# A two-layer expert stage with its first layer turned round: tokens on partitions, 512 weight columns as the moving operand, rows transposed by DMA

## The chip, the cores and the metric

The kernel runs on one core of a Trainium2 chip. Its engines are TensorE (PE: matmuls, with PEld for the weight loads), VectorE (DVE), ScalarE (ACT), GpSimd (POOL) and SyncE (SP). Each works through its own instructions in order and waits on semaphores that other engines or DMAs raise. DMAs are issued from the queues of SP, ACT and POOL; a DMA transpose is issued from SP here. A matmul multiplies a stationary operand (at most 128 x 128, the "weights" of the instruction, lhsT) with a moving operand of up to 512 columns (rhs), and adds into a PSUM bank of 512 fp32 columns. The metric is the device time of one execution in microseconds.

## What is computed

Attention over 4 batches, 8 heads, 768 positions and 64 dimensions per head is followed by a mixture of 4 experts. Three heads attend to all earlier positions, five to 4 sink positions and a window of 64. The 3072 x 512 result, one row per token, goes through every expert:

```python
p = domain_probs / (domain_probs.sum(-1, keepdims=True) + 1e-09)
out = np.zeros((N, D), dtype=np.float32)          # N = 3072 tokens, D = 512
for e in range(E):                                # E = 4 experts, F = 1024
    h = np.maximum(x @ w1[e], 0.0)                # layer 1: 512 -> 1024
    out += p[:, e:e + 1] * (h @ w2[e])            # layer 2: 1024 -> 512
```

Since a probability is positive, p * max(h, 0) = max(p * h, 0): the probability may be applied before the second layer. Both kernels do that in the stage that the change touches.

## The kernel before

Tokens are handled in 24 tiles of 128. Attention works in 8 groups of three tiles (half a batch each, `attention(b, c)`) and leaves its result transposed, in `xT[g]`: model dimension on partitions (4 chunks of 128), tokens on the free axis. Attention of the first group runs alone. Then `moe_steps` is a generator of expert work, and a loop at the end of the kernel weaves steps of the remaining attention between its steps by a plan of spent time. All engines' orders are as the program emits them; nothing is reordered by a scheduler.

Tiles 0 to 3 go through the experts in a plain way. The other 20 tiles go in ten *pairs* (`pair_steps`), and these pairs are the subject here. A pair has 256 tokens.

*Layer 1 before.* The hidden units are put on partitions: the stationary operand is a 128 x 128 block of w1, the moving operand is 256 token columns of `xs`, the inputs already multiplied by the probability (`scale_inputs`, L1158, on DVE; the probabilities come broadcast over partitions as `pB`, 512 KB per pair, by DMA from a scratch array `p_rows`). `plain_layer1` (L1207) does 8 x 4 matmuls per expert and evicts on ACT with Relu (L1216) into `hA`, in five blocks: A11, A21, A12, A22 (tokens of tile 0 or 1, hidden units of the lower or upper half) and S1. In this layout a block can be used directly as the stationary operand of layer 2.

*Half products.* Some experts' layer 1 is done by `winograd_layer1` (L1236): seven products of half size instead of eight, by the Winograd form of Strassen's scheme, with sums of inputs (`scaled_sums`) and of weights (`first_weight_sums`, in `t1`) prepared on DVE, and intermediate results kept by ACT (L1246) and added by DVE (L1253). In the first seven pairs one expert of four goes this way, in the eighth two, in the ninth three, in the last all four. Each such product is 8 matmuls of 128 columns.

*Layer 2.* Both experts' and tokens' halves go through the same scheme once more: seven products of 16 matmuls with 256 columns (L1387), accumulating over the four experts at once. The sums S1 = A21 + A22 (`first_sum`), S2 = S1 - A11, S3 = A22 - S2, S4 = A12 - S2 are made by DVE (L1182, L992), mostly in place over A11, A21 and A12. ACT keeps intermediate results (L1407), DVE adds them (L1410), SP stores the output (L1417).

*Queues.* SP issues, in program order, the loads of `pB` (L1135), the output stores, the transposes of keys and queries for the next attention group (`transpose_rows`, L263, six of 128 x 512 per group), and two transposes of attention results per group (L768, `x_one` and `x_pair`, 128 x 384). POOL issues the loads of weights, keys, queries and values.

Of the kernel before, what the change touches and what calls it, by code (L numbers as in the profile page):

```python
# [19 lines left out]
def kernel(  # L20
# [34 lines left out]
    P = 128  # L55
# [62 lines left out]
    kR = []  # L118
    vR = []
    for i in range(2):  # L120
        kR.append(pers.tile([P, NCH, NR, 3, P], FP16, name=f"kR{i}"))
        vR.append(pers.tile([P, S // P, NR, D + 2], FP16, name=f"vR{i}"))
# [27 lines left out]
    probs = pers.tile([P, NPL, E], FP32, name="probs")  # L150
    psums = pers.tile([P, NPL], FP32, name="psums")
    p_sb = pers.tile([P, NPL, E], FP32, name="p_sb")
    p_all = moe.tile([P, 2 * E * P], FP32, name="p_all", tag="o", bufs=1)
    p_in = p_all[0:NTILE, 0 : E * P].rearrange("t (x e) -> t x e", e=E)
    p_out = p_all[0:NTILE, E * P : 2 * E * P].rearrange("t (e x) -> t e x", e=E)
    r_rows = moe.tile([P, P], FP32, name="r_rows", tag="sums", bufs=1)[0:NTILE, :]


# [19 lines left out]
    def key_tile(b, c, h, t):  # L178

        i = b % 2  # L180
        if RETR[h]:
            return kR[i][:, t // 3, RH.index(h), t % 3, :]
        if b:
            return windows(kSf)[:, t, SH.index(h), :]
        return kS[:, t // TC, t % TC, SH.index(h), :]
# [72 lines left out]

    def transpose_rows(b, c):
        alloc_qT(b, c)  # L260
        for x, xr, at in ((kT, k_rows[b, c], P), (qTs[b, c], q16[b, c], 0)):
            for j in range(3):
                nc.sync.dma_start(  # L263
                    out=x[:, :, at + j * P : at + (j + 1) * P],
                    in_=xr[:, j, :, :].rearrange("p h d -> p (h d)"),
                    transpose=True,
                )
# [3 lines left out]
    def keys_to_rows(b, c):  # L271

        for n, hps in ((slice(0, 2), slice(0, 2)), (slice(2, 3), slice(3, 4))):
            nc.vector.tensor_copy(
                out=kR[b % 2][half(0), c, n, :, :].rearrange("p n t x -> p n (t x)"),
# [64 lines left out]
    def in_pairs(e):  # L340

        return e < 2

    def w1_tile(e, ct, ft):

        return w_tile(e, w1sb[:, e * DMP + ct, :], ft)

    def w_tile(e, x, ft):
        if in_pairs(e):
            x = x[:, ft // 2 * 2 * P : (ft // 2 + 1) * 2 * P]  # L350
            return x.rearrange("p (x j) -> p j x", j=2)[:, ft % 2, :]
        return x[:, ft * P : (ft + 1) * P]

    def load_w2(e):
        x = w2sb[:, e * FTP : (e + 1) * FTP, :]
        if in_pairs(e):
            gp.dma_start(
                out=x.rearrange("p (m j) d -> p m (j d)", j=2),
                in_=moe_w2[e].rearrange("(m p j) d -> p m (j d)", p=P, j=2),
            )  # L360
            return
# [44 lines left out]
    for h in range(H):  # L406
# [18 lines left out]
    nc.sync.dma_start(  # L425
        out=probs,
        in_=moe_domain_probs[0 : NPL * P, :].rearrange("(t p) e -> p t e", p=P),
    )
    nc.sync.dma_start(
        out=p_in.rearrange("t x e -> t (x e)"),  # L430
        in_=moe_domain_probs.rearrange("(t x) e -> t (x e)", x=P),
    )
# [6 lines left out]
    zero(nc.vector, kR[0][:, 0, :, :, :])  # L439
# [73 lines left out]
    zero(gp, kR[0][:, 1, :, :, :])  # L513
    zero(gp, kS[:, 1, :, :, :])
    one_values(gp, 1)
    k16 = moe.tile([P, H, 3, D], FP16, name="k16", tag="pB", bufs=1)
# [41 lines left out]
    def attention(b, c):  # L558
# [8 lines left out]
        def transposes(hp):  # L567
            for x, is_k in ((q32 if first else qt16, 0), (k32 if first else k16, 1)):
# [22 lines left out]
                for u in range(2):  # L591
                    h = 2 * hp + u
                    r = slice(u * D, (u + 1) * D)
                    if RETR[h]:
                        nc.vector.tensor_copy(  # L595
                            out=rows_in_order(
                                kR[i][r, c, RH.index(h), :, :].rearrange(
# [289 lines left out]
        else:  # L887
# [37 lines left out]
            if more:  # L925
                if g == 1:
                    load_probs(pair0)
                    transpose_rows(*more)
            for h in waiting:
# [3 lines left out]
    def small_things():  # L933
# [8 lines left out]
        normalise(probs, psums, p_sb)  # L942

    def normalise(x, sums, out):
# [5 lines left out]
        for e in range(E):  # L950
            nc.vector.tensor_tensor(
                out=out[:, :, e], in0=x[:, :, e], in1=sums, op=ALU.mult
            )


    p_rows = tc.dram_tile([NTILE, E * P], FP32, name="p_rows")
    pair0 = NPL

    def prob_rows():
        normalise(p_in, r_rows, p_out.rearrange("t e x -> t x e"))  # L960
        nc.sync.dma_start(out=p_rows.rearrange("t (e x) -> t e x", e=E), in_=p_out)

# [13 lines left out]
    hA16 = hA  # L976
    blocks = hA.rearrange("p (b k x) -> p b k x", b=5, k=KT)
    A11, A21, A12, A22, S1 = (blocks[:, n, :, :] for n in range(5))
# [27 lines left out]
    t1 = {(EW[0], n): t1sb[:, n, :, :] for n in range(3)}  # L1006
# [9 lines left out]

    def room_for_more_sums():

        x = kR[0].rearrange("p c n t x -> p (c n t x)")
        y = att.tile([P, KH * FN], FP16, name="t1", tag="k_rows", bufs=1)  # L1020
        for n in range(3):
            z = x[:, n * KH * FN : (n + 1) * KH * FN] if n < 2 else y
            t1[EW[1], n] = z.rearrange("p (c f) -> p c f", c=KH)
        x = att.tile([P, DMP * PC], FP16, name="xs1", tag="q16", bufs=1)
        own_room[EW[1]] = x.rearrange("p (c x) -> p c x", c=DMP)

    EW3 = E - 3

    def room_for_third():

        n = KH * FN
        for i in range(3):
            t1[EW3, i] = vSf[:, i * n : (i + 1) * n].rearrange("p (c f) -> p c f", c=KH)

    def room_for_fourth():

        n = KH * FN
        x = [vSf[:, 4 * n : 5 * n], kSf[:, 2560 : 2560 + n]]
        x.append(xs_of[0][:, DMP * PC : 2 * DMP * PC])
        for i, y in enumerate(x):  # L1040
            t1[0, i] = y.rearrange("p (c f) -> p c f", c=KH)

# [603 lines left out]
```

## Time and profile before

Three runs took 376.20, 376.30 and 376.58 us, the median is 376.3 us. The profiled execution has a span of 374.9 us from its first instruction to its last, 1.4 us under the median; what lies around the span is not in the profile. Where the stages lie in it:

| stretch, us | what runs | length, us |
|---|---|---|
| 0 to 41.0 | first attention group, weights arrive, first expert begins | 41.0 |
| 41.0 to 87.8 | tiles 0 to 3 through the experts, second attention group | 46.8 |
| 87.8 to 295.9 | pairs 1 to 7, woven with attention groups 3 to 8 | 208.1 |
| 295.9 to 322.4 | pair 8 (two experts by half products), no attention | 26.5 |
| 322.4 to 347.6 | pair 9 (three) | 25.2 |
| 347.6 to 374.9 | pair 10 (four) and the last stores | 27.3 |

Over the span the busy shares are PE 98%, PEld 83%, DVE 76%, ACT 61% and POOL 30%; the granted clock of TensorE is full. Busy times of matmuls are modelled, since matmuls overlap: the distance from one start to the next is what a matmul costs. A group's row gives its line, engine, operation, operands and shapes, then its count, total and mean time, and after the last bar how long the engine had been idle before it and who ended that. A row of SP in the timeline (SPq) is an issue of a DMA, not the transfer.

### The profile page before, as it was taken

Reading aid. Unit: us, or ns where it says so; the run is one execution under the profiler, and the core shown is the slowest. Engines: PE = TensorE matmul, PEld = TensorE weight load, DVE = VectorE, ACT = ScalarE, POOL = GpSimd, SP = SyncE. Lnnn points to the kernel's source line nnn. Section 1 sums busy time; section 2 is a strip of 40 time slices with the busy share of each in tenths; the row PEclk is TensorE's granted clock in tenths of the full one; section 3 lists DMA queues with packets and bytes.
Section 4 is the critical chain, followed back from the end, with each engine's and each line's share of the span. In section 5 each row is a group of like instructions: output and inputs, shape, how many; then the busy total and the mean of one; then the engine's idle time right before and its main releaser. Section 6 shows DMA issues by size and latency. Waiting matters only on the chain.

```text
span 374.9 us, 10290 instructions
## 1 busy us (share of the span) xinstructions
PE 367.2 (98%) x4200; PEld 310.5 (83%) x4200; DVE 284.3 (76%) x610; ACT 227.2 (61%) x475; POOL 113.1 (30%) x155
## 2 busy tenths in 40 slices
PE   8899999999999999999999999999999999999996
PEld 4755466668998988999989898998899998998996
DVE  7775768697788669868658858957767868989882
ACT  3863478547785785765676955784777361450630
POOL 8924573872057038115601650320000000000000
PEclk9999999999999999999999999999999999999999
DMA  8999999999599599988904990951220300300101
GB/s 163 158 202 208 197 183 192 183 201 110 97 111 155 94 97 116 159 111 61 208 10 61 170 158 15 125 134 14 71 69 3 104 13 0 115 2 3 57 2 58
DMA packets 123748, 39.25 MB, mean 105 GB/s; under 512 B 113728, under 2 KB 116356, under 8 KB 123700
## 3 DMA queue, kind: packets, MB, share of 16 engines
q0 software_dynamic: 85824, 19.01, 58.8%
q1 hardware_dynamic: 36276, 19.18, 21.9%
q8 instruction: 33, 0.54, 0.6%
q10 hardware_dynamic: 1600, 0.39, 0.5%
q14 instruction: 15, 0.12, 0.1%
HBM read 44.89 MB, written 6.34 MB: 137 GB/s over the span
## 4 chain that ended last, share of the span: by engine, by line
PE 87%; DMA 7%; POOL 3%; DVE 1%; ACT 0%; issue 0%; POOLq 0%
PE pO L1387 31%; PE pA L1207 22%; PE pO L1236 9%; DMA w2sb<-in_moe_w_dram 7%; PE pO L1094 6%; PE pA L678 5%; PE pA L1073 5%; PE pV L1236 2%; PE pV L734 2%; PE pA L1236 2%; PE pV L806 2%; POOL vS L310 1%; POOL vR L304 1%; DVE xs L1158 1%; PE pA L1479 0%; POOL early L472 0%
## 5 line engine op out<-in xcount | busy, mean ns | idle before, releaser
L1387 PEld LDWEIGHTS <-hA 128*128 128x128 f16 x1104 | 104.9, 98 | 12.2
L1207 PE MATMUL pA<-xs,w1sb 128*128 128x256 f16 x768 | 97.2, 272 | 0.0
L1207 PEld LDWEIGHTS <-w1sb 128*128 128x128 f16 x768 | 71.8, 98 | 7.6
L1387 PE MATMUL pO<-w2sb,hA 128*128 128x256 f16 x640 | 76.7, 272 | 0.0
L696 ACT ACTIVATE es<-pA 128x384 f16<-128x384 f32 (+2 forms) x122 | 59.2, 512 | 27.1 <-PE pA L678 23.3
L1216 ACT ACTIVATE hA<-pA 128x512 f16<-128x512 f32 x96 | 57.2, 597 | 29.0 <-PE pA L1207 26.7
L306 POOL DMA_DIRECT2D vS<-in_v_dram x30 | 29.6, 986 | 111.9 <-PE pV L806 110.6
L1387 PE MATMUL pO<-tsb,hA 128*128 128x256 f16 x464 | 56.7, 272 | 0.0
L1158 DVE TENSOR_TENSOR xs<-xT,pB 128x1024 f16<-128x1024 f16 (+1 forms) x49 | 47.0, 978 | 1.4 <-DMA xT<-x_pair 1.4
L992 DVE TENSOR_TENSOR hA<-hA 128x1024 f16<-128x1024 f16 x60 | 39.5, 685 | 0.4
L1086 ACT ACTIVATE hA<-pA 128x384 f16<-128x384 f32 (+1 forms) x64 | 22.2, 385 | 19.4 <-PE pA L1073 18.7
L1236 PEld LDWEIGHTS <-w1sb 128*128 128x128 f16 x512 | 31.4, 98 | 1.4 <-issue 0.5
L1073 PE MATMUL pA<-xT,w1sb 128*128 128x384 f16 (+1 forms) x256 | 31.1, 273 | 0.7 <-DVE xT L829 0.3
L1094 PE MATMUL pO<-w2sb,hA 128*128 128x512 f16 x128 | 30.7, 379 | 0.3 <-DMA w2sb<-in_moe_w_dram 0.3
L1407 ACT COPY s<-pO 128x256 f32<-128x256 f32 x31 | 11.5, 372 | 27.7 <-PE pO L1387 21.9
L829 DVE TENSOR_TENSOR xT<-pV,rc 64x384 f16<-64x384 f32 x37 | 20.5, 555 | 10.3 <-ACT rc L834 7.9
L1073 PEld LDWEIGHTS <-w1sb 128*128 128x128 f16 x256 | 19.4, 98 | 9.7 <-issue 1.5
L824 ACT ACTIVATE rc<-pV,eps 64x384 f32<-64x384 f32 x37 | 21.3, 575 | 6.5 <-PE pV L806 5.9
L700 DVE TENSOR_TENSOR es<-es,mS 128x384 f16<-128x384 f16 (+1 forms) x40 | 13.7, 344 | 15.0 <-ACT es L696 15.0
L1246 ACT COPY s<-pO 128x512 f32<-128x512 f32 x39 | 22.7, 587 | 3.2 <-PE pO L1236 3.0
L1253 DVE CUSTOM_DVE_ANT_0 hA<-pO,s 128x512 f16<-128x512 f32 x26 | 17.7, 688 | 7.7 <-PE pO L1236 6.3
L678 PE MATMUL pA<-qT,kR 128*128 128x384 f16 (+2 forms) x120 | 22.9, 278 | 0.7 <-DVE kR L595 0.6
(170 smaller groups left out, 528.0 us busy)
## 6 DMA issues: line engine op xcount, KB each, us to landing
pB<-p_rows SPq DMA_DIRECT2D x10, 512.0 KB
out_dram<-o SPq DMA_DIRECT2D x19, 256.0 KB
w1sb<-in_moe_w_dram POOLq DMA_DIRECT2D x8, 512.0 KB, 9.2
w2sb<-in_moe_w_dram POOLq DMA_DIRECT2D x4, 1024.0 KB, 12.3
vS<-in_v_dram POOLq DMA_DIRECT2D x30, 112.0 KB, 4.3
k_rows<-in_k_dram POOLq DMA_DIRECT2D x18, 128.0 KB, 5.2
q<-in_q_dram POOLq DMA_DIRECT2D x18, 128.0 KB, 6.4
vR<-in_v_dram POOLq DMA_DIRECT2D x24, 48.0 KB, 5.8
```

The lines of the kernel that those rows point to most:

```text
L306: gp.dma_start(out=t[:, :, own_v(h)], in_=windows_of(v, b, h, c))
L678: nc.tensor.matmul(out=ps[:, o : o + nq], lhsT=key_tile(b, c, h, t), rhs=qTs[b, c][:, hp, q0 : q0 + nq], start=(n == 0 or not first), stop ...
L696: nc.scalar.activation(out=es[:, 0:cols], in_=ps[:, 0:cols], func=AF.Exp, scale=SC)
L992: nc.vector.tensor_tensor(out=out, in0=a, in1=b, op=ALU.subtract)
L1073: nc.tensor.matmul(out=pss[ft][:, 0:cols_n], lhsT=w1_tile(e, ct, ft), rhs=x[:, ct, :], start=(n == 0), stop=(n == DMP - 1),)
L1094: nc.tensor.matmul(out=ps_o, lhsT=hs[:, ft, j * P : (j + 1) * P], rhs=w2sb[:, e * FTP + ft, :], start=(ft == 0), stop=(ft == FTP - 1),)
L1158: nc.vector.tensor_tensor(out=o, in0=xin, in1=pb.to_broadcast([P, DMP, n, P]), op=ALU.mult)
L1207: nc.tensor.matmul(out=ps[:, f * PC : (f + 1) * PC], lhsT=w1_tile(e, ct, f0 + f), rhs=xs[:, ct, :], start=(ct == 0), stop=(ct == DMP - 1),)
L1216: nc.scalar.activation(out=blocks[:, b0 : b0 + 2, k0 : k0 + 2, :].rearrange("p t f x -> p f t x"), in_=ps.rearrange("p (f t x) -> p f t x" ...
L1236: nc.tensor.matmul(out=ps[:, f * P : (f + 1) * P], lhsT=w_tile(e, w[:, ct, :], f), rhs=a[:, ct, :], start=(first and f == 0 and ct == 0), ...
L1246: nc.scalar.copy(out=kept[n], in_=ps)
L1387: nc.tensor.matmul(out=ps, lhsT=a[:, k, :], rhs=b(k), start=(first and k == 0), stop=(k == KT - 1), skip_group_check=not first,)
```

## The change

Only the pairs' first layer and what feeds it are rewritten; the second layer keeps its seven products.

- *Layer 1 is turned round.* The stationary operand is a 128 x 128 block of `xT` itself (dimension x tokens), the moving operand 512 columns of w1. A result has tokens on partitions and 512 hidden units on the free axis. A step of `plain_layer1` (called n in the prediction) is 4 matmuls of 512 columns into one bank.
- *The probability is a scalar per partition.* Evictions multiply by it (`relu`, with `scale=` on ACT or as a tensor_scalar on DVE). `scale_inputs`, `p_rows` and the loads of `pB` go.
- *DMA transposes the rows.* A finished row of 128 tokens x 1024 hidden units goes back to the layout that layer 2 needs by `to_blocks`, one DMA transpose of eight 128 x 128 blocks on SP. There are eight per pair (four experts, two tiles). Four row buffers are used in turn (`new_row`).
- *Two experts by half products.* The first pair does one expert that way, the other nine two (EW = experts 3 and 2; their generators are a and b). A half product is 2 matmuls of 512 columns. The kept results and the sums carry the probability; a `clip` on DVE does the Relu of three of the four quarters. The input sums (`x_sums`) are made once per pair, since inputs are no longer scaled per expert.
- *Orders.* In pairs 2 to 10 the steps go: n; a a n; a a n; a a n; a b; b n; b b n; b b n; b n. Layer 2 takes the experts in the order 0, 3, 2, 1 and begins with the first twelve matmuls of its first product (experts 0, 3, 2), the first twelve of its second, and then the last four of each.
- *Around it.* The six transposes of keys and queries are put in a list (`sp_jobs`) and issued one per step of layer 2, or all at the start of the next attention group. The key tile `kR` exists once instead of twice, w2 of experts 0 and 1 loses its pairing of rows, and the special storage of the last three pairs goes.

```diff
     def transpose_rows(b, c):
...
-                nc.sync.dma_start(
...
+                sp_jobs.append(
+                    functools.partial(
+                        nc.sync.dma_start,
...
+    rows = []
+    n_row = itertools.count()
+
+    def new_row():
+        if not rows:
+            x = moe.tile([P, 3, F], FP16, name="rows", tag="xs", bufs=1)
+            x_sum(2)
+            y = more_x[0][:, 0:2, :].rearrange("p a x -> p (a x)")
+            rows.extend([x[:, 0, :], x[:, 1, :], x[:, 2, :], y])
+        return rows[next(n_row) % len(rows)]
+
+    def to_blocks(row, e, i):
+        n0 = (2 * e + i) * F
         nc.sync.dma_start(
+            out=hA[:, n0 : n0 + F].rearrange("p (k x) -> p k x", x=P),
+            in_=row,
+            transpose=True,
         )
...
-        def plain_layer1(e):
-            xs = scaled(e)
-            for f0 in range(0, FTP, 2):
...
+        def relu(eng, out, ps, i, e):
+            if eng is nc.scalar:
+                eng.activation(out=out, in_=ps, func=AF.Relu, scale=scale_of(i, e))
+            else:
+                eng.tensor_scalar(
+                    out=out, in0=ps, scalar1=scale_of(i, e), scalar2=0.0,
+                    op0=ALU.mult, op1=ALU.max,
+                )
+
+        def plain_layer1(e, by_vector=()):
+            for i in range(PT):
+                row = new_row()
+                for j in range(2):
                     ps = bank()
                     for ct in range(DMP):
                         nc.tensor.matmul(
+                            out=ps,
+                            lhsT=x_of(nt0 + i, ct),
+                            rhs=w1sb[:, e * DMP + ct, j * FN : (j + 1) * FN],
                             start=(ct == 0),
                             stop=(ct == DMP - 1),
                         )
+                    eng = nc.vector if 2 * i + j in by_vector else nc.scalar
+                    relu(eng, row[:, j * FN : (j + 1) * FN], ps, i, e)
+                    if j == 1:
+                        to_blocks(row, e, i)
+                    yield DMP * mm_ns(FN), 0.5
...
+        def winograd_layer1(e, x, y):
+            ns = KH * mm_ns(FN)
+            rows = [new_row() for _ in range(PT)]
...
+            product(x, w1_part(e, 0, 0), x_part(nt0, 0, 0), True)
+            keep(0, x, 0)
             yield ns, 0.5
             z = bank()
+            product(z, w1_part(e, 1, 0), x_part(nt0, 0, 1), True)
+            add(0, z, 0, 0)
             yield ns, 0.5
+            product(x, t(1), x_sum(1), False)
+            keep(1, x, 0)
             yield ns, 0.5
+            product(y, t(0), x_sum(0), True)
+            keep(2, y, 1)
             yield ns, 0.5
+            product(x, w1_part(e, 0, 1), x_sum(2), False)
+            add(2, x, 1, 1)
             yield ns, 0.5
+            product(y, w1_part(e, 1, 1), x_sum(3), False)
+            add(1, y, 0, 1)
+            clip(rows[0])
+            to_blocks(rows[0], e, 0)
+            clip(block(1, 1))
             yield ns, 0.5
+            product(x, t(2), x_part(nt0, 1, 1), False)
+            relu(nc.scalar, block(1, 0), x, 1, e)
+            to_blocks(rows[1], e, 1)
             yield ns, 0.5
...
+            n = itertools.chain(plain_layer1(0, (3,)), plain_layer1(1, (1,)))
             order = (
+                ((n,), None),
+                ((a, a, n), None),
+                ((a, a, n), None),
+                ((a, a, n), None),
+                ((a, b), None),
+                ((b, n), None),
+                ((b, b, n), lambda: first_sum(slice(0, 1))),
+                ((b, b, n), lambda: first_sum(slice(3, 4))),
+                ((b, n), None),
             )
+            experts = (0, 3, 2, 1)
...
+        def ns(k):
+            if sp_jobs:
+                sp_jobs.pop(0)()
+            return k * mm_ns(HN), PSHARE
+
+        product(x, A11, b(0, 0), True, 0, K3)
+        yield ns(K3)
+        product(y, A12, b(1, 0), True, 0, K3)
+        second_sum(0)
+        yield ns(K3)
+        product(x, A11, b(0, 0), True, K3, KT)
         keep(0, x)
+        yield ns(HT)
+        product(y, A12, b(1, 0), True, K3, KT)
         add(0, y, 0, 0)
+        for e in experts[2:]:
+            first_sum(slice(e, e + 1))
+        second_sum(1)
+        yield ns(HT)
+        product(x, S2, t(1), False, 0, K2)
...
+        if nxt is not None:
+            x_sums(nxt)
```

In the changed kernel layer 1's matmuls stand at L1145 (plain) and L1169 (half products), the evictions at L1132 (ACT) and L1134 (DVE), the keeps at L1179, the adds at L1187, the clips at L1193, `to_blocks` at L1112, first_sum at L1119, and layer 2's matmuls at L1280.

## The prediction

> **What bounds the kernel now.** I read the page first: busy times, the row of granted clock, the chain that ended last.
>
> ```profile
> PE 367.2 (98%) x4200; PEld 310.5 (83%) x4200; DVE 284.3 (76%) x610; ACT 227.2 (61%) x475; POOL 113.1 (30%) x155
> PEclk9999999999999999999999999999999999999999
> PE 87%; DMA 7%; POOL 3%; DVE 1%; ACT 0%; issue 0%; POOLq 0%
> ```
>
> TensorE is busy for 98% of the span at the full clock, and the chain is 87% TensorE. So the time is its streaming time, and anything that makes it wait is added. Next the chain in order of time, for the true cadence (busy times there are modelled longer):
>
> ```profile
> 43.50 0.86 PE pO L1094 x4
> ...
> 298.78 0.87 PE pA L1207 x8
> 299.65 0.89 PE pO L1236 x16
> ...
> 309.36 12.23 PE pO L1387 x112
> ```
>
> These are back-to-back runs: 216 ns for a matmul of 512 columns, 109 for 256, 56 for 128. Layer 2 of a pair is 112 matmuls, 12.2 us. The last three pairs have no attention, so they stand bare; the windows by stage (columns: window, length, PE busy, PEld, DVE, ACT, POOL, PEclk, DMA, GB/s) show how little they lose:
>
> ```profile
> 295.90:322.40 26.50, 26.50 (x307) 24.45 (x306) 20.82 (x42) 10.99 (x22) 0.00 (x0) 1.00 0.15 51
> 322.40:347.60 25.20, 25.20 (x315) 23.48 (x313) 21.84 (x44) 10.13 (x21) 0.00 (x0) 1.00 0.12 44
> ```
>
> The second, pair 9, has 12.9 us of layer 1 by the cadences (32 x 0.109 + 168 x 0.056) and 12.2 of layer 2: 25.1 of its 25.2. There is no stall left to remove. Then the groups, for what evicts and sums (mean ns of one after the comma):
>
> ```profile
> L1216 ACT ACTIVATE hA<-pA 128x512 f16<-128x512 f32 x96 | 57.2, 597 | 29.0 <-PE pA L1207 26.7 <-PE pV L734 0.9
> L992 DVE TENSOR_TENSOR hA<-hA 128x1024 f16<-128x1024 f16 x60 | 39.5, 685 | 0.4
> L1110 DVE SCALAR_TENSOR_TENSOR hA<-pO,p_sb,hA 128x512 f32<-128x512 f32 x12 | 9.0, 749 | 2.3 <-PE pO L1094 2.1
> L290 DVE COPY kS<-kT 64x1736 f16<-64x1736 f16 x12 | 7.7, 644 | 0.3
> L1182 DVE TENSOR_TENSOR hA<-hA 128x512 f16<-128x512 f16 x12 | 5.0, 421 | 1.2 <-ACT hA L1216 1.0
> L298 DVE COPY kT<-kT 128x320 f16<-128x320 f16 x5 | 1.2, 244 | 0.1
> ```
>
> Last the timeline of SP and DVE, for the transposes that exist today:
>
> ```profile
> 123.69 1.19 SPq L768 DMA_TRANSPOSE xT<-x_one  x1
> 131.50 3.83 SPq L263 DMA_TRANSPOSE kT<-k_rows  x3
> 241.65 1.21 SPq L768 DMA_TRANSPOSE xT<-x_pair  x1
> 245.13 1.29 DVE L1158 TENSOR_TENSOR xs<-xT,pB 128x512 f16<-128x512 f16 x2 [1.38 <-DMA xT<-x_pair]
> ```
>
> A transpose holds SP for 1.2 us, the same for three 128x128 blocks (x_one) as for four (kT), and three in a row go out every 1.31 us. The x_pair one of 241.65 freed DVE at 245.1, 3.4 us later, behind six others. The quiet one of 123.69 completed at 126.05 by its completion events: 2.35 us, of which 1.2 are issue, 0.6 its 384 packets and 0.55 completion.
>
> **What the change saves.** Layer 1 of the pairs is now 768 matmuls at 109 ns and 896 at 56, 133.9 us. After it: 62 of 512 columns in the first pair and 60 in each of nine others, 602 x 216 ns = 130.0. Saved 3.9 us, all on the path. The scaling of inputs goes (L1158, 52 instructions, about 50 us of DVE) with ten 512 KB loads of pB: off the path, worth nothing by itself. The dropped pairing of w2 rows changes packets from 2048 to 1024 bytes; in the trace both kinds move 207 GB/s, so the early w2 wait (0.44 us at 38.4) stays. If they went at half that rate, expert 1's w2 would be 5 us late there.
>
> **What it adds.** Eight transposes of 128x1024 per pair (to_blocks), 80 in all, on SP. No row has eight blocks. Issue: 1.25 us, from three and four blocks alike; if it grows with blocks, 2.45. Packets: 1024 over 16 DMA engines, 64 each at the 18 ns of a packet plus 0.2 of ramp, 1.35 us; completion 0.55. So 3.15 us from issue to landing is my value. The ends: 2.35, if the larger one costs no more than the small, and 4.4 with the longer issue.
>
> DMA: Bandwidth & Descriptors, "Latency and other measured facts", gives 261 GB/s for a transpose with a strided middle dimension. The trace has less: kT's 512 packets, 128 KB, pass in 0.76 us, 172 GB/s. By the page's figure 256 KB would take about 1.0 us, and an estimate of the time would fall by some 6 us.
>
> **Where they end up on the path.** I follow a bare pair from its layer 1 start, in us. Steps: n (plain, 4 matmuls) 0.86, a and b (half products, 2 matmuls) 0.43. PE to ACT or DVE takes 0.2 (352.66 in the trace). ACT evicts 512 columns every 0.51. A DVE add from PSUM costs 0.75, a clip of 1024 about 0.44 (between L298 and L290; at L992's rate 0.69, which would lengthen stalls 1 and 2 by 0.25 each).
>
> *Stall 1, row buffers.* There are four rows. Counting new_row: expert 0 takes rows 0 and 3, a takes 1 and 2, b takes 0 and 1, expert 1 takes 2 and 3. So step n5 (expert 1, first half) is evicted by ACT into row 2, which a's second transpose is still reading. a6 ends at 5.2; its add queues behind the one of a5, then clip: 6.8. SP then issues in order: a's first row 6.85 to 8.1, expert 0's second row 8.15 to 9.4 (DVE had evicted it by 7.75), a's second row, ready since 7.3, 9.45 to 10.7. It lands at 12.6. ACT wanted to evict n5 at 8.4 and stands until 12.6; queued behind it are the keeps of b3 and b4, which b5 and b6 need before they accumulate in the same banks. b5 starts at 13.8 instead of 9.9: with b6, 4.0 us.
>
> *Stall 2, layer 2's third expert.* Layer 2 starts at 16.95. b's first row is added and clipped by 16.3 and lands at 19.5; layer 2 reads it at its ninth matmul, 17.8: 1.7 us.
>
> *Stall 3, DVE's run.* After the second product ends, DVE does add (0.42), two first_sums (0.42 each), second_sum (0.69) in order; overlapping a little, 2.0 us with the hand-over, against 0.87 of matmuls: 1.1 us. It needs no slow DMA.
>
> Sum 6.8 us in pairs 8 to 10. In pairs 2 to 7 the emitted order puts attention matmuls into these places, on average 0.3, 0.45 and 0.8 us; I let them cover 1.4: 5.4. The first pair has one such reuse (expert 1's second row on a's first), about 1.4 with free banks covering the rest. Total 3 x 6.8 + 6 x 5.4 + 1.4 = 54.2, less 3.9: +50.3. On the span, 374.9 becomes 425.2; the median run is 1.4 us over the profiled span, so **426.6**.
>
> With landing 2.35 the stalls are 3.2, 0.9, 1.1: 15.6 + 22.8 + 1.0 - 3.9 = +35.5, 412. With the longer issue they are 7.0, 2.3, 2.7: 36 + 63.6 + 3 - 3.9 = +99, 475. I take the middle because isolated packets and issue times both fit it.
>
> The trace's longest pause between matmuls after the first 5 us is 1.2 us, with the clock at 1.00 in every window. TensorE: Matmul & The Clock Gate, "What's actually happening", says that an idle window of about 3.4 us halves the clock for the next one. Stall 1 would be the first pause near that; by the page up to 1.7 us more per pair, an estimate of 15 us, against nothing by the rows; no run here shows it yet.
>
> **Other parts, costed at nothing.** ACT: 14 evictions and keeps in 13 us of layer 1 at 0.51 is 7.1, covered by its idle (29 us before L1216). The 36 kT and qT transposes now go one per layer 2 step instead of in one burst. SP then carries some 16 issues of 1.3 us per pair of 30: it fits. If a job stands behind a to_blocks that waits, keys_to_rows on DVE waits for kT and holds masks and adds: 2 to 3 us at each of five groups. x_sums (four of 0.28) run beside the last product. One kR for two costs nothing, as a batch's scores are over before the next one's keys are copied.
>
> **The rivals.** *A, short landing*: the transposes cost what a small one does. For it: the fixed part dominates in three and four blocks. Against: packets are real work. 400 to 416. *B, transposes back up*: issue grows with blocks, or v loads, which keep the DMA engines at eight or nine tenths in most slices up to 243 us, share them. For: 3.4 us for x_pair. Against: issue is equal for three and four blocks. 438 to 480. *C, the other side, hidden*: a transpose issues like a plain DMA (pB: 0.33 us) and lands 1.5 us after its relu, before ACT needs row 2. Then stalls 1 and 2 vanish, and it is faster where stall 3 is below 3.9/9 = 0.43 us per pair: 372.4 with none, 380 with all of it. Against: 1.2 us of issue in every transpose row. That the half products save nothing is no rival: the matmul count is fixed.
>
> **How the numbers follow.** My forecast 0.56 (own range 416 to 438), A 0.20, B 0.14, C 0.10, of which 0.06 faster, 0.01 the same, 0.03 slower. The range 400 to 452 takes the forecast, nearly all of A and under half of B. Slower by over 0.2% (about what a measurement tells here): 0.56 + 0.20 + 0.14 + 0.03 = 0.93.
>
> **What would show it.** Right: ACT at L1132 idle on a DMA from rows for about 4 us once per pair; TensorE waiting at L1169 on ACT, and at L1280 on a DMA and then on DVE; bare pairs of 32 us; matmuls of 512 at 216 ns. Wrong: transposes that hold SP for far less or more than 1.25 us, a clock below 1.00, or first waits on SP behind an attention transpose.

## The result, and the profile after

The changed kernel takes 475.8 us (474.2 to 477.8) against 376.4: a ratio of 1.2635, 95% interval 1.2598 to 1.2672. It is slower, as forecast, but by 99 us where 50 were predicted, and outside the range of 400 to 452. The profiled execution spans 472.5 us. Where the executions of a kernel below lie more than 1.5% above its fastest, its ratio is of the others alone: one execution of the last experiment took 768.8 us, the other three 408 to 410.

The page of the changed kernel: busy times, granted clock, and the chain that ended last.

```profile
PE 392.4 (83%) x3138; PEld 249.7 (53%) x3138; DVE 262.0 (55%) x605; ACT 227.8 (48%) x457; POOL 112.9 (24%) x154
PEclk9999999997997999998899589979989989979989
PE 49%; DMA 22%; DVE 9%; ACT 8%; SPq 4%; issue 4%; POOL 3%; ACTq 0%; DVEq 0%; POOLq 0%
```

TensorE is no longer nearly the whole chain: it is 49% of it, and DMA, DVE, ACT and SP are 43%. The clock, a row of nines before, has dips from the first pair on. Four of the same page's groups (mean ns of one after the comma, then the idle time before them and what ended it):

```profile
L1280 PE MATMUL pO<-w2sb,hA 128*128 128x256 f16 x640 | 79.1, 275 | 4.2 <-DMA hA<-rows 4.2
L1280 PE MATMUL pO<-tsb,hA 128*128 128x256 f16 x464 | 58.2, 273 | 11.8 <-DVE hA L972 9.8
L1169 PE MATMUL pO<-w1sb,xs 128*128 128x512 f16 x76 | 27.2, 476 | 44.9 <-ACT s L1179 44.9
L1132 ACT ACTIVATE rows<-pA,p_sb 128x512 f16<-128x512 f32 x35 | 23.8, 687 | 69.9 <-DMA hA<-rows 63.5
```

These are the three stalls by name. ACT stands 63.5 us in front of its evictions into rows until a transpose has read the row; TensorE then stands 44.9 us at b's products behind ACT's keep (stall 1), 4.2 at layer 2 on the row itself (stall 2), and 9.8 on DVE's second_sum (stall 3). The chain in order of time, for pair 9, the bare pair that starts at 402.5:

```profile
410.78 1.28 SPq L1112
...
412.15 3.07 DMA hA<-rows
...
415.90 0.69 ACT s L1179
...
416.63 1.87 PE pO L1169 x4
...
426.34 0.42 DVE o L1299
...
427.01 0.43 DVE hA L1119
...
427.47 0.70 DVE hA L972
...
428.21 8.03 PE pO L1280 x72
```

In the timeline, ACT's eviction into the row stands before the keep of 415.90:

```profile
415.32 0.69 ACT L1132 ACTIVATE rows<-pA,p_sb 128x512 f16<-128x512 f32 x1 [4.89 <-DMA hA<-rows]
```

SP issues expert 0's second row at 410.78, a's second row at 412.15, and this lands 3.07 us later (predicted: 3.15). ACT, idle for 4.89 us until then, evicts and keeps, and b5 starts at 416.63 after a pause of 4.2 us (predicted: 4.0). The four matmuls from there take 1.87 us instead of 0.86: half clock. Below, stall 3 is the predicted run of add, first_sums and second_sum. Windows of pair 9 and, under it, pair 8 (columns as before):

```profile
402.50:436.10 33.60, 28.61 (x175) 17.40 (x173) 14.38 (x29) 10.34 (x18) 0.00 (x0) 0.90 0.38 79
369.90:402.50 32.60, 27.48 (x175) 17.07 (x173) 14.28 (x29) 10.34 (x18) 0.00 (x0) 0.95 0.40 81
```

These two bare pairs take 33.6 and 32.6 us, near the 32 forecast. So most of the 49 us that are missing lie elsewhere. Counted is what a pair takes beyond the full-clock cadence of its matmuls, waits and half clock together. Against the prediction's own sums that is +9.8 us in pair 1, +32.8 in pairs 2 to 7 and +3.4 in pairs 8 to 10; 2.0 more go before the first pair. These are 48.0 us; the spans of the two profiles leave 47.3 to explain.

In pair 1 lines of the timelines of SP and of ACT show two waits where one was counted:

```profile
99.79 1.75 SPq L754 DMA_TRANSPOSE xT<-x_one  x1
101.63 11.56 SPq L1112 DMA_TRANSPOSE hA<-rows  x4
104.81 1.26 ACT L1132 ACTIVATE rows<-pA,p_sb 128x512 f16<-128x512 f32 x2 [5.81 <-DMA hA<-rows]
...
110.67 1.26 ACT L1132 ACTIVATE rows<-pA,p_sb 128x512 f16<-128x512 f32 x2 [3.64 <-DMA hA<-rows]
```

Expert 1's second row waits for a's first (5.81 us), and expert 2's first for a's second (3.64). In pair 5 the same wait of ACT is 10.8 us, in pair 9 it was 4.9 (lines of the timelines of POOL and of SP around it, then ACT's waits in that stretch):

```profile
256.36 2.68 POOL L213 DMA_DIRECT2D q<-in_q_dram  x3
258.22 3.20 SPq L1112 DMA_TRANSPOSE hA<-xs  x1
259.00 2.32 POOL L307 DMA_DIRECT2D vR<-in_v_dram  x3
```

```profile
ACT rows L1132 <- DMA hA<-rows: 10.8, 1, 10.8
```

Here the k, q and v loads of the next attention group run over layer 1; SP's issue takes 3.2 us instead of 1.28.

### The profile page after: what moved, and what is told of

It reads as the page before. It is cut to its first block, busy times and chain, and to the rows that moved or that the text cites. A ratio compares the mean times of both kernels' runs of the same rounds, so it can differ in the third digit from the quotient of the medians.

```text
span 472.5 us, 8342 instructions
## 1 busy us (share of the span) xinstructions
PE 392.4 (83%) x3138; PEld 249.7 (53%) x3138; DVE 262.0 (55%) x605; ACT 227.8 (48%) x457; POOL 112.9 (24%) x154
## 4 chain that ended last, share of the span: by engine, by line
PE 49%; DMA 22%; DVE 9%; ACT 8%; SPq 4%; issue 4%; POOL 3%; ACTq 0%; DVEq 0%; POOLq 0%
PE pO L1280 21%; DMA hA<-rows 12%; PE pA L1145 8%; PE pO L1169 8%; SPq L1112 4%; DMA q<-in_q_dram 4%; PE pO L1041 4%; DMA w2sb<-in_moe_w_dram 3%; PE pA L1020 3%; DVE rows L1187 3%; ACT s L1179 2%; PE pA L664 2%; DVE hA L972 2%; DMA w1sb<-in_moe_w_dram 2%; DVE hA L1119 2%
## 5 line engine op out<-in xcount | busy, mean ns | idle before, releaser
L1280 PEld LDWEIGHTS <-hA 128*128 128x128 f16 x1104 | 104.5, 98 | 36.0 <-DVE hA L972 12.3
L1145 PE MATMUL pA<-w1sb,xT 128*128 128x512 f16 x336 | 97.1, 416 | 7.9 <-ACT rows L1132 5.5
L1280 PE MATMUL pO<-w2sb,hA 128*128 128x256 f16 x640 | 79.1, 275 | 4.2 <-DMA hA<-rows 4.2
L682 ACT ACTIVATE es<-pA 128x384 f16<-128x384 f32 (+2 forms) x122 | 59.3, 512 | 36.3 <-PE pA L664 31.6
L1280 PE MATMUL pO<-tsb,hA 128*128 128x256 f16 x464 | 58.2, 273 | 11.8 <-DVE hA L972 9.8
L1169 PE MATMUL pO<-w1sb,xs 128*128 128x512 f16 x76 | 27.2, 476 | 44.9 <-ACT s L1179 44.9
L1145 PEld LDWEIGHTS <-xT 128*128 128x128 f16 x336 | 34.4, 105 | 49.5 <-issue 22.0
L1132 ACT ACTIVATE rows<-pA,p_sb 128x512 f16<-128x512 f32 x35 | 23.8, 687 | 69.9 <-DMA hA<-rows 63.5
L972 DVE TENSOR_TENSOR hA<-hA 128x1024 f16<-128x1024 f16 x60 | 39.4, 687 | 13.9 <-PE pO L1280 13.4
L1169 PEld LDWEIGHTS <-xs 128*128 128x128 f16 x76 | 7.8, 107 | 56.4 <-issue 51.7
L1187 DVE SCALAR_TENSOR_TENSOR rows<-pO,p_sb,s 128x512 f16<-128x512 f32 x38 | 27.6, 748 | 17.8 <-PE pO L1169 9.9
L1179 ACT ACTIVATE s<-pO,p_sb 128x512 f32<-128x512 f32 x57 | 36.9, 685 | 0.2
L686 DVE TENSOR_TENSOR es<-es,mS 128x384 f16<-128x384 f16 (+1 forms) x40 | 13.8, 346 | 34.0 <-ACT es L682 33.9
L1132 ACT ACTIVATE xs<-pA,p_sb 128x512 f16<-128x512 f32 x31 | 21.4, 691 | 23.1 <-PE pA L1145 23.0
L1299 DVE TENSOR_TENSOR o<-pO,s 128x256 f32<-128x256 f32 x30 | 12.7, 423 | 25.7 <-PE pO L1280 15.1
```

What stands on the lines that cost most here:

```text
L682: nc.scalar.activation(out=es[:, 0:cols], in_=ps[:, 0:cols], func=AF.Exp, scale=SC)
L972: nc.vector.tensor_tensor(out=out, in0=a, in1=b, op=ALU.subtract)
L1132: eng.activation(out=out, in_=ps, func=AF.Relu, scale=scale_of(i, e))
L1145: nc.tensor.matmul(out=ps, lhsT=x_of(nt0 + i, ct), rhs=w1sb[:, e * DMP + ct, j * FN : (j + 1) * FN], start=(ct == 0), stop=(ct == DMP - 1),)
L1169: nc.tensor.matmul(out=ps, lhsT=a[:, ct, :], rhs=w[:, ct, :], start=(first and ct == 0), stop=(ct == KH - 1), skip_group_check=True,)
L1179: nc.scalar.activation(out=kept[n], in_=ps, func=AF.Copy, scale=scale_of(i, e))
```

## The experiments

Three questions: is stall 1 what the prediction says it is (rows, SP's queue, landing); where do the 49 us come from (loads, attention, half clock); and can the new order be made cheap enough to beat the kernel before? Bare pairs are pairs 8 to 10. From first matmul to first matmul pairs 8 and 9 took 25.5 and 25.1 us before (the 26.5 of the first table hold 1 us of pair 9); pair 10 ends with the last stores, 28.4 us before and 36.4 after, and is not meant where a length is given.

**A fifth row buffer** in the space of the output tile, rows given by hand so that n5 and b never take a row in flight.

```
+            {0: (0, 3), 3: (1, 2), 1: (0, 4), 2: (3, 0)}
+            if first
+            else {0: (0, 3), 3: (1, 2), 2: (4, 1), 1: (0, 3)}
...
-                row = new_row()
+                row = plan_rows[e][i]
+                row = fifth if row == 4 else row_of(row)
```

> A fifth row buffer in the space of the output tile, and rows given out by hand, so that no eviction writes a row whose transpose has just been issued. Theory (row buffers make ScalarE stand, and the pause halves the clock): the pause before b5, 51.6 us over the ten pairs, is gone and the clock stays near 1.00 (21 us back); stall 2 grows to about 1.8 us a pair, stall 3 stays at 1.1; 405 to 420 us, bare pairs of about 28 us. Rival (the transposes are limited by throughput, of SP or of the DMA engines): the waiting moves to layer 2, TensorE at L1289 on DMA, and the time stays at 455 to 476.

437.5 us, ratio 1.163 (1.158 to 1.169): 38 us back, between the two. The wait before b5 is gone and bare pairs take 29.7 us. What pair 1 loses falls from 11.2 to 4.8. Waits of TensorE in the bare pairs (us in all, times, longest):

```profile
PE pO L1289 <- DMA hA<-o: 6.0, 3, 2.0
PE pO L1180 <- DVE rows L1198: 2.7, 3, 1.0
PE pO L1289 <- DVE hA L972: 2.6, 3, 0.9
```

Stall 1 is the row buffers, but stall 2 rises to 2.2 us a pair, and a wait of 1.0 before b7 appears: DVE's add stands behind a first_sum that waits for expert 0's second row.

**Fifteen independent matmuls in the pause before b5**, to hold the clock.

```
-                ((b, b, n), lambda: first_sum(slice(0, 1))),
+                ((b, b, n), lambda: (first_sum(slice(0, 1)), keep_busy())),
```

> Fifteen matmuls of 512 columns that depend on nothing (3.2 us, into a spare bank, result unused) are put before b5 in pairs 2 to 10; all waits stay. Theory (a pause of TensorE over about 3.4 us halves its clock): the clock returns to about 1.00 in the bare pairs, TensorE's pause there is about 1 us, and the time falls by 8 to 18 us, to 458 to 468. Rival (the half clock hides under waits that exist anyway, or does not come from the pause): 474 to 480.

479.3 us, ratio 1.274 (1.271 to 1.277): the rival. Pairs 8 and 9 run at full clock now (granted 1.00, pair 10 0.98) and are as long as in the changed kernel, 33.6 and 32.7 us. What the fill does not cover of the pause stays, 1.0 to 1.9 us, and stall 2 grows to 1.8.

**No k, q and v loads for batches 2 and 3.**

```
     def load_q(b, c):
+        if b >= 2:
+            q16[b, c] = q16[1, 1]
+            return
```

> The loads of keys, queries and values for the attention groups of the last two batches are left out (old data is used again); all else stays. Theory (attention's loads share the DMA engines with the transposes and lengthen their landing): in pairs 4 to 7 the pause before b5 comes down to the 4.2 us of the bare pairs, from 3.9, 10.0, 6.6 and 4.1, and some clock comes back; 460 to 467 us. Rival (attention's exponentials queue on ScalarE behind the eviction that stands, whatever the loads): pauses as before, 473 to 477.

466.4 us, ratio 1.239 (1.237 to 1.241), as the theory has it: 9.4 us. ACT's wait in pair 5, in its own line:

```profile
ACT rows L1140 <- DMA hA<-rows: 5.2, 1, 5.2
```

10.8 has become 5.2, and TensorE's pause there 4.4 instead of 10.0; in pair 6 it is 5.3 instead of 6.6. Bare pairs are unchanged.

**No transposes from pair 2 on.**

```
+        if next(n_tr) >= 8:
+            return
         nc.sync.dma_start(
```

> The transposes to blocks are issued in the first pair alone; in the other nine the rows are computed and never transposed, and layer 2 works on what is there. All other work stays. Theory: stalls 1 and 2 and the half clock vanish from pairs 2 to 10, stall 3 (the run of sums on VectorE) stays at about 1 us a pair; 376.3 - 3.9 + 2 for the start + 10 for the first pair + 9 x 0.8 = 392, between 385 and 396. Rival (the turned layer is slow by itself, in its evictions or its 512-column matmuls): over 405.

406.1 us, ratio 1.079 (1.076 to 1.082): on the rival's side by its time, though not for the rival's reason, since the waits and pair 1 make up the difference. So the transposes of pairs 2 to 10, with all that follows from them, cost 70 of the 99 us. The other 30 us are there without them: pair 1, which keeps its transposes, is 13 us longer than before; pairs 2 to 7 have 1.9 to 3.4 us of waits each, small ones at half products behind attention's work on ACT and DVE, and stall 3; a bare pair takes 26.7.

**SP's order alone**: expert 0's second row is issued behind a's second.

```
-                    if j == 1:
+                    if j == 1 and (e, i) == (0, 1) and not first:
+                        held.append(row)
+                    elif j == 1:
                         to_blocks(row, e, i)
...
             to_blocks(rows[1], e, 1)
+            if held:
+                to_blocks(held.pop(), 0, 1)
```

> One edit on SP alone: from pair 2 on, the transpose of expert 0's second row is issued behind that of the second row of a instead of before it; everything else is as in the changed kernel. Theory (the transposes go out one after another, 1.27 us of SP each, and ACT's n5 eviction waits for the last of three): the pause before b5 falls by one issue in every pair, in the bare pairs from 4.2-4.35 to about 3.0 us, and with it under the 4 us at which the half clock was seen; bare pairs 30.5 to 32.0 us (32.6 to 33.6 before the edit), whole kernel 455 to 466. Rival (the landing is set by the DMA engines or by the rows, not by SP's order): the pause stays over 3.9 us and the time at 472 to 478.

460.0 us, ratio 1.221 (1.219 to 1.223), as the theory has it. The pause before b5 is 3.0 us in all bare pairs; two of them keep the full clock, and pair 10 loses it after the same pause. ACT's eviction in pair 9:

```profile
403.11 0.69 ACT L1135 ACTIVATE rows<-pA,p_sb 128x512 f16<-128x512 f32 x1 [3.69 <-DMA hA<-rows]
```

3.69 us against 4.89: one issue of 1.27 us less. SP's queue is a part of the landing.

**Layer 2's order of experts**, so that b's late row comes last; alone, and with the fill.

```
-            experts = (0, 3, 2, 1)
+            experts = (0, 3, 1, 2)
```

> Layer 2 of pairs 2 to 10 takes its experts in the order 0, 3, 1, 2 instead of 0, 3, 2, 1, so that the half products' late first row (b) is read at the 25th matmul of layer 2 instead of the 9th: stall 2 alone is taken away (in the changed kernel it stands at 0 to 1.9 us, 5.1 in all). Theory (half the clock costs its full 1.4 to 3 us per pair, and stall 2 only looks small because the slow matmuls hide it): stall 2 goes, the rest stays, 469 to 473. Rival (the late row is waited for at the next place, by DVE's sum): 474 to 478.

476.1 us, ratio 1.265 (1.263 to 1.267): no gain, the rival.

> The same order of experts and the fifteen independent matmuls in the pause before b5. This fill alone gave 479.3 us: it kept the clock up, but stall 2 grew to 1.8 us in the bare pairs. Theory (the half clock was paid for by stall 2; with stall 2 gone the full clock shows as time): bare pairs 31.0 to 31.8 us, whole kernel 460 to 467, which is 5 to 10 us under the kernel with the order alone. Rival (the clock was never worth anything, another late row takes its place): 473 to 480, no faster than the order alone.

Ratio 1.261 (1.253 to 1.268), 475 us: no gain either. TensorE's waits in layer 2 of the bare pairs, first with the fill alone, then with both (an execution of 480.5 us):

```profile
PE pO L1291 <- DMA hA<-rows: 4.9, 3, 1.6
PE pO L1291 <- DVE hA L972: 2.6, 3, 0.9
```

```profile
PE pO L1291 <- DVE hA L972: 6.7, 3, 2.4
```

Stall 2 has become stall 3. They are one wait for layer 1's last rows, met at the first place that needs them, and a faster TensorE only meets it earlier.

**The fifth row and the new order together.**

> The fifth row buffer (437.5 us alone, stall 1 gone from b5, but stall 2 of 0.3 to 2.2 us in every pair, 16 us in all) with the order 0, 3, 1, 2. Theory (stall 2 is the wait for b's first row alone): bare pairs 27.4 to 27.9 us (29.65 with the fifth row alone), whole kernel 421 to 427. Rival (the second rows land as late, and DVE's two first_sums and second_sum wait for them): stall 3 grows from 1.0 to 2.5 us or more, 431 to 438.

440.1 us, ratio 1.166 (1.159 to 1.173): the rival's mechanism, at 2 us over its range. Stall 3 is 2.2 to 2.6 us.

**Transposes on a second queue**: ACT issues second rows whose last relu is its own.

```
-            to_blocks(rows[1], e, 1)
+            to_blocks(rows[1], e, 1, nc.scalar)
```

> The changed kernel with the transpose of every second row whose last relu is ACT's (a's, b's, expert 1's; in the first pair the plain experts' too) issued from ACT's own queue instead of SP's; rows, order and sums stay. Theory (the landing is 3.2 us, and what makes it late is SP, where three transposes of 1.27 us queue up): a's second row is under way 2 us earlier, the pause before b5 falls from 4.2-4.35 to 2.2-2.8 us, bare pairs 29.5 to 31.0 us, whole kernel 436 to 452. Rival (the transposes queue up behind one another wherever they are issued, or ACT's 1.27 us per issue costs as much as it brings): 465 to 480.

529.4 us, ratio 1.407 (1.404 to 1.410): far worse than either expected. The timeline of ACT in pair 9, then SP's largest wait for transposes, over the whole span (us in all, times, longest):

```profile
457.03 0.69 ACT L1132 ACTIVATE rows<-pO,p_sb 128x512 f16<-128x512 f32 x1 [1.46 <-PE pO L1169]
460.45 1.25 ACTq L1112 DMA_TRANSPOSE hA<-rows  x1
...
463.60 0.69 ACT L1132 ACTIVATE rows<-pA,p_sb 128x512 f16<-128x512 f32 x1 [1.16 <-DMA hA<-rows]
```

```profile
SPq L1112 <- DMA hA<-rows: 61.0, 10, 9.4
```

a's second row is ready at 457.7 and goes out at 460.45, when the transposes that SP issued have landed; and at this line alone SP waits 61 us for transposes to land; with one queue its transposes wait for none. On one queue transposes follow every 1.3 us; across two, each waits for the other's landing. These are waits of the program. The Trainium skill, DMA: Bandwidth & Descriptors, "Latency and other measured facts", says why they must be there: two transposes in flight from different queues corrupt each other's output silently, and software has to serialize them. No run here tried them without.

> The fifth row buffer and the order 0, 3, 1, 2 (440.1 us, stall 3 of 2.2 to 2.6 us in the bare pairs) with those second rows' transposes on ACT's queue. Theory (stall 3 waits for the last of three transposes that SP issues from 384.0 on in pair 9, the third 2 us after its relu): stall 3 falls to 0.4 to 1.1 us, bare pairs 27.0 to 28.0 us, whole kernel 422 to 430. Rival (two queues are no faster): 436 to 444.

538.1 us, ratio 1.427 (1.420 to 1.435): the same loss, and again worse than either expected.

**Layer 2's middle reordered** (S2 first half, S1, S2 second half, S4 first half, S3, S4 second half), so that the second_sum is needed 1.75 us later; first on that kernel, then with POOL's loads issued one per step of layer 2, then on SP's queue alone.

```
         product(x, S2, t(1), False, 0, K2)
...
+        product(y, S1, t(0), True, 0, K2)
...
+        product(y, S1, t(0), True, K2, KT)
...
         product(x, S2, t(1), False, K2, KT)
...
-        product(y, S1, t(0), True, 0, K2)
...
-        product(y, S1, t(0), True, K2, KT)
```

> The same with layer 2's middle reordered: S2 first half, S1 both halves, S2 second half, S4 first half, S3 both, S4 second half, one first_sum of two experts instead of two, and the first halves of the third and fourth sums ahead of the add on DVE. The second_sum that stall 3 waits for is needed 1.75 us later. Theory: stall 3 goes to under 0.3 us, bare pairs 26.2 to 27.0 us, whole kernel 5 to 10 us under the kernel without this step. Rival (the next wait, for a keep on ACT or a bank, takes its place): within 2 us of it.

526.5 us, ratio 1.398 (1.396 to 1.400): 12 us less than without, a little more than the theory's 5 to 10.

> The same with the nine loads of k, q and v for the next attention group issued by POOL one per step of layer 2 instead of in one burst, which lay in layer 1 of pairs 4 to 6. Leaving two batches' loads out gave 9.4 us. Theory (the burst shares the DMA engines with the transposes that layer 1 waits for): 5 to 10 us faster than the kernel without this step, gained in pairs 4 to 6. Rival (layer 2's own transposes, or the attention that waits for k and q, pay for it): within 2 us of it or slower.

524.8 us, ratio 1.395 (1.390 to 1.400): no difference that the intervals show.

> The fifth row buffer, the order 0, 3, 1, 2 and the reordered middle of layer 2 (S2 first half, S1 both halves, S2 second half, S4 first half, S3 both, S4 second half; one first_sum of two experts), all transposes on SP's queue. Without the reordered middle: 440.1 us, stall 3 of 2.2 to 2.6 us in the bare pairs. Theory (the second rows land when they land, and only the distance to their first use counts; it grows by 0.9 us for the first_sum and 1.75 for the second_sum): stall 3 falls to 0.3 to 1.4 us, bare pairs 27.2 to 28.2 us, whole kernel 424 to 432. Rival (another wait takes its place): 436 to 442.

423.7 us, ratio 1.125 (1.122 to 1.129): the theory, 16 us less than the 440.1. What the bare pairs still wait for (pairs 8 and 9 take 27.4 and 27.9 us):

```profile
PE pO L1180 <- DVE rows L1198: 2.7, 3, 0.9
PE pO L1289 <- DVE hA L1119: 2.1, 3, 0.9
PE pO L1289 <- DMA hA<-o: 1.3, 3, 0.8
```

**Fewer, larger transposes**: both rows of an expert in one of sixteen blocks, of b, of a and b, of a alone.

```
+            if both(e):
+                to_blocks(row_at(plan_rows[e][0], 2), e, 0, 2)
```

> The same with a sixth row buffer and both rows of b transposed by one instruction of sixteen blocks instead of two of eight: one issue less in layer 1's tail, as many bytes. Theory (an issue costs 1.25 us whatever the number of blocks, three, four and eight being alike, so the last row leaves SP one issue earlier): expert 1's second row lands about 1 us earlier, 4 to 9 us faster than without the merge. Rival (an issue of sixteen blocks takes 2.5 us, or b's rows land so much later that the third expert's wait comes back): within 3 us of it, or slower.

428.6 us, ratio 1.138 (1.135 to 1.141): slower. Pair 9's issue and the matmul that waits for it:

```profile
379.45 1.95 SPq L1114 DMA_TRANSPOSE hA<-o  x1
...
383.84 1.05 PE L1307 MATMUL pO<-w2sb,hA 128*128 128x256 f16 x8 [1.66 <-DMA hA<-o]
```

Sixteen blocks hold SP for 1.95 us, not 1.25, and the eight issued right behind them 1.7, not 1.27, so that the two instructions take 3.65 us of SP where three of eight took 3.8. Layer 2 goes on 4.4 us after the issue of the sixteen began, where eight land after 3.0 to 3.2.

> Both rows of a merged too, so that six transposes are issued per pair instead of eight. In the bare pairs a wait of 1.0 us before b7 was left: DVE stands on expert 0's second row, behind a's first on SP, before it can add b's block. Theory (SP's queue is what makes that row late): the wait before b7 goes, 5 to 9 us faster than with b's rows merged alone. Rival (a's rows, later by the merge, are waited for by DVE's sum of expert 3): the same within 2 us, or slower.

423.6 us, ratio 1.124 (1.122 to 1.127): 5 us better than with b's alone; the wait before b7 is halved to 0.5 us, not gone.

> Both merges, and POOL's nine loads of k, q and v for the next attention group one per step of layer 2 instead of in a burst over layer 1 of pairs 4 to 6. Theory (the burst shares the DMA engines with the transposes that layer 1 waits for; leaving two batches' loads out gave 9.4 us): 5 to 10 us faster than with the burst, gained in pairs 4 to 6. Rival (on the kernel with ACT's queue the same step gave 1.7 us; layer 2 or the attention pays): within 3 us of it. Whole kernel then 400 to 425 us, above the kernel before by either theory.

Ratio 1.118 (1.116 to 1.120), 421 us: 2.5 us less than with the burst, the rival's side.

> Six row buffers, the order 0, 3, 1, 2, the reordered middle of layer 2, and only a's two rows transposed by one instruction of sixteen blocks. With both merges: 423.6 us, with none: 423.7. Theory (in the bare pairs the merge of a takes 0.5 us from the wait before b7, the merge of b makes layer 2 wait 0.9 us longer for b's rows): the best of the three, bare pairs 27.0 to 27.5 us, whole kernel 416 to 421. Rival (the gains of one place are waited for at the next): 422 to 426.

420.6 us, ratio 1.118 (1.111 to 1.124): within the theory, though the interval reaches into the rival's range, and level with the 421 before it. These two are the best that compute everything. A bare pair, in windows:

```profile
361.10:388.00 26.90, 25.86 (x174) 16.54 (x172) 14.67 (x28) 10.35 (x18) 0.00 (x0) 1.00 0.47 97
```

26.9 us against 25.1 to 25.5 before: by the cadences the matmuls alone take 25.2, as before, and the waits that are left take 1.8.

> The same with the k, q and v loads of batches 2 and 3 left out (their attention then runs on old data; the rest is computed as before). In the changed kernel this gave 9.4 us, in pairs 4 to 6. Theory (what is left over the bare pairs' rate in pairs 4 to 6 is the sharing of the DMA engines): 8 to 12 us faster, the wait before b7 of pair 5 from about 4.5 to 1 us. Rival (with other waits shorter the loads are hidden): within 3 us.

Ratio 1.086 (1.082 to 1.089), 409 us: 11 us less, the theory by its time. Where it lay is not shown, since the profile is of the execution of 768.8 us.

## Why the prediction was wrong

The mechanism forecast for the bare pairs is there, with nearly its size. What failed is the step from them to the other pairs: the attention's cover, then the first pair's single reuse, and the clock, which the sum left at nothing.

*What the change saves*, 3.9 us on the path: not contradicted; matmuls of 512 columns run at 216 ns where the clock is full.

*Issue and landing*: right. 1.23 to 1.29 us and 3.0 to 3.2 in the bare pairs, predicted 1.25 and 3.15. Rival A's 2.35 and rival B's longer issue are refuted for eight blocks. That the measured 475.8 us lies on the sum with the longer issue, 475, and in rival B's range is therefore chance. The packets of a transpose alone on the queue (416.15) pass in 1.41 us, 186 GB/s; the sum had 1.35. By the 261 GB/s that the Trainium skill, DMA: Bandwidth & Descriptors, "Latency and other measured facts", has for a transpose with a non-contiguous middle dimension, an estimate is 1.0 us, and the landing would have been 0.4 us shorter than it was.

*Stall 1, row buffers*: right in mechanism, place and size: 4.2 to 4.35 us in bare pairs against 4.0, and the order on SP step by step. The swap and the fifth row show both of its causes.

*Stall 2, layer 2's third expert*: 0 to 0.9 us in bare pairs, not 1.7. Behind stall 1 layer 1 ran at half clock, and the row had more time to land; at full clock, with the fill and with SP's order changed, it was 1.8. *Stall 3, DVE's run*: 1.03 us, and 0.23 ahead of the add, against 1.1. But these two are not separate terms: take one away and the other grows, as the reordered experts showed.

*The attention's cover*: this step failed. "I let them cover 1.4: 5.4" made pairs 2 to 7 cheaper than bare ones. They lost 8.0 to 16.1 us each to waits and half clock, 65.2 in all instead of 32.4. Of the 32.8, 8.4 is the cover itself. 8.8 is stall 1 longer than 4.0, nearly all of it in pairs 5 and 6, where the loads run beside the transposes (rival B's second clause, right in these pairs; leaving the loads out gave 9.4). 6.4 is waits at half products: 2.5 of it, in pair 4, behind a DVE that waits for a row to land, which goes without the loads; the rest, in kind, stays when no transpose is left. 12.2 is half clock, whose price is open (below). Stalls 2 and 3, at 13.4 instead of 16.8, give 3.4 back, and pauses too short to name make up the rest.

The small cover of stall 1, 0.3, is about there: 3.8 to 4.4 us in pairs 2, 3, 4 and 7. What is missing is the cover of stalls 2 and 3: 2.2 us a pair, against 1.5 in bare pairs, where 0.45 and 0.8 had been taken off. Attention matmuls that stand in line at the place of a wait had been counted as cover; but what TensorE waits for can itself stand behind the attention's share on ACT and DVE. At stall 3 of pair 4 the chain runs over an attention exponential on ACT (L682) and its mask on DVE (L686) before the sums that end with the second_sum (L972):

```profile
235.13 0.51 ACT es L682
...
235.67 0.07 DVE es L686
...
237.00 0.70 DVE hA L972
```

How much of the missing cover is due to this no run shows.

*The first pair*, "one such reuse, about 1.4": 11.2 us, 3.1 of them half clock. Four buffers for eight rows make four reuses; two of them waited: the order there has plain experts behind a, and SP carries an attention transpose between (1.75 us at 99.79). With the hand-made plan of five rows layer 1 of pair 1 has no wait left.

*The clock*: the sum took "nothing by the rows" for it, and named a clock below 1.00 as a sign of being wrong. It came: half clock in every pair, 21.2 us of stretched matmuls in all (pair 1 3.1, pairs 2 to 7 12.2, bare 6.0). As an event this was foretold by the estimate of 15 us from the Trainium skill, TensorE: Matmul & The Clock Gate, "What's actually happening". As a price it is not shown: the fill kept the clock up in the bare pairs and won nothing (103.1 us for the three against 102.7), since stall 2 grew. In pairs 2 and 3, too, the fill brought the full clock: 4.2 us of stretched matmuls went, and the two took 75.3 us instead of 75.8. For pairs 4 to 7, where the fill left some half clock, it stays open.

*Before the first pair*, w2 "costed at nothing": 2.0 us. Waits for w1 grew by 0.8 us and those for w2 by 0.3; the rest was not traced to a cause.

*The other side* (rival C, hidden) is refuted: with six rows, a's two transposes in one and a reordered layer 2, 44 us remain: 29 in pairs 2 to 7, 8 in pair 1, 6 in pairs 8 to 10, 1 before them; 11 of the 44 go with the loads. Nothing tried came below the kernel before.

## What to carry to other kernels

Ask of a transfer in a short loop not only when its data are needed, but when its source buffer is: here a fifth row buffer, which changes the reuse alone, took away 38 of the 70 us that the transposes cost. Waits on rows of one late queue are one wait with several places; add them up only after asking which is left when the first is gone. Do not credit other work with cover because its instructions stand there: see whether it runs on the very engines and queues that are late.

## What the runs showed of the hardware

*The clock follows a fixed grid.* Half-clock records begin on a grid of 3.413 us. Against the program's first instruction the grid lay at another place in every profile, by 0.3 to 3.2 us. I split eighteen profiles (the changed kernel and all experiments but the last) along it, from 5 us on. A window's pause is the time in it that no matmul covers, a matmul counted at its start-to-start time (216 ns for 512 columns, 427 at half clock). Of full-clock windows with under 2.0 us of pause, 0 of 1932 were followed by half clock; with 2.15 us or more, 147 of 147; between, 10 of 23. Of windows at half clock with under 0.8 us of pause, 155 of 156 were followed by full clock; with more, 2 of 99. So a pause need not last a whole window: 2.15 us can be enough if they fall inside one, and 3.0 us were harmless in two bare pairs of three. The Trainium skill, TensorE: Matmul & The Clock Gate, "What's actually happening", names an idle window of about 3.4 us; the grid agrees with it, and the share that makes a window idle is what these runs add.

*A transpose's issue is not flat*: 1.2 us for three or four blocks, 1.23 to 1.29 for eight, 1.5 to 2.2 for sixteen with 1.6 to 2.0 for the eight right behind them; landing 2.35 us after the issue began for three, 3.0 to 3.2 for eight, 4.3 to 4.4 for sixteen. Beside a burst of loads the issue of eight took 3.2 us.

*ACT's eviction* with a scale per partition took 0.69 us for 128x512, against 0.60 without it before; back to back they started every 0.59 us, against 0.49.
